# Block attention followed by a Fourier mixing layer: q and k of the last head pairs loaded in 32x32 blocks and turned on VectorE

## The chip, the cores and the metric

The kernel runs on one core of a Trainium2 chip. The metric is the device time of one execution in microseconds (us). The kernel before took 298.1 us, the median of three runs (297.7 to 298.16).

## What is computed

The reference has two halves, and the second works on the output of the first.

```python
# 1. block-sparse causal attention: B=4, H=8, S=768, D=64, blocks of 64 keys, top 3 blocks
k_rep = k.reshape(B, H, 12, 64, D).mean(axis=3)
gate  = einsum('bhsd,bhnd->bhsn', q, k_rep)          # which key blocks a query may see
mask  = (top-3 blocks of gate  |  own block) & causal
attn  = softmax(where(mask, q @ k.T / sqrt(D), -1e9))
x     = (attn @ v), heads side by side               # [4, 768, 512]
# 2. Fourier mixing and a two-layer net
mixed = real(fft(fft(x, axis=1), axis=2))
u     = x + mixed
un    = (u - mean(u)) / sqrt(var(u) + 1e-6)
out   = u + relu(un @ w_ch1) @ w_ch2                 # w_ch1 [512, 2048], w_ch2 [2048, 512]
```

## The kernel before

**Pairs and batches.** Attention is worked off in 16 head pairs `P` (0 to 15, four to a batch `b`). A pair is two heads of 64 numbers side by side, so that its transposed q and k fill 128 partitions. When the four pairs of a batch are done, the batch goes through the Fourier half and the two matrix products, W1 (16 steps `w:b,it`) and W2 (12 steps `c:b,st,h`). The attention of later batches is laid between the products of earlier ones.

**One order, written out by hand.** The string `ORDER` lists some thousand steps, each a short name with its arguments. The loop at the end calls them in that order, and the schedule is manual for all five queues (SyncE, called SP; TensorE, PE; VectorE, DVE; ScalarE, ACT; GpSimd, POOL). Each engine therefore works off its own instructions in the order in which the string names them and stops at the first one whose inputs are not there. Nothing reorders at run time. Between engines only semaphores hold.

**The steps of a pair.** `Lk`, `Lq` and `Lv` load k, q and v of a pair (function `load`, issued on SP: two DMAs each for k and q, line 275, one for v, line 270). The tile `nat0` (q) and `nat1` (k) hold tokens on the partitions and come in three buffers each. `tk` and `tq` (`a_tp`, line 292) turn them on PE: six transposes of 128x128 each against the identity, from fp32 SBUF into one PSUM tile `tp`. `ks` (line 297, DVE) sums k over each block of 64 tokens out of that PSUM tile; `kh` spreads the sums; `kc` (lines 308 and 311, ACT) writes k in fp16 into `qk`. `qc` (line 316, DVE) copies q from PSUM to the fp32 tile `q32`; `qs` (POOL) writes it in fp16 into `qk`. Then come the gate `g` (PE, from `q32` and the sums), the choice of blocks `gt`, `gx`, `gl`, `gm` (DVE), `K` (POOL, the mask rows of `qk`), the scores `s` (PE, lines 409 and 414), `e` (ACT, line 431, the exponential), `d` (POOL, line 437, the causal corner), `vc` (POOL, v to fp16), `v` (PE, line 449, attention times values) and `x` (DVE, the division).

**The steps of a batch.** `fs`, `fd`, `f` (DVE) fold `x`; `y` and `m` (PE) are the two Fourier products; `ty` (ACT) and `tr` (DVE, line 538) move the first product's result out of PSUM; `u` (DVE, line 566) adds; `xu` (ACT, line 578) centres the rows in fp16. `un` turns them into `unT`, for batch 0 by PE and DVE, for the other batches by two DMA transposes per step on the SP queue (line 593). `bn`, `nv`, `nr` are the statistics. `w` (PE, lines 629 and 631) is W1, `r` its ReLU (ACT, line 641; every fourth one DVE, line 639), `c` (PE, line 656, for the last piece line 648) is W2, `o` (DVE, line 668) adds, and `od` (SP, line 673) writes 128 rows of the output.

**Buffers that tie the queues together.** All PSUM tiles come from one pool of four. `u` has five buffers for three tiles a batch, so that later batches wait for earlier `od`. A DMA on SP takes one of eight completion lanes and waits until the DMA eight places before it has landed.

The part of the order that the change leaves as it is ends behind the first normalised rows of batch 0 (step `bn:0,3`); W1 of batch 0 begins there, some 59 us into the execution.

Of the kernel before, what the change touches and what calls it, by code (L numbers as in the profile page):

```python
# [116 lines left out]
qs:3 ks:3 s:1,4 e:1,0 tq:4 d:0,1 gx:2 vc:0 e:1,4 s:1,3 qc:4 s:1,1 Lv:2 e:1,3 s:1,2 gl:2,0 kh:3  # L117
tk:4 gl:2,1 e:1,2 d:1,3 gm:2 g:3 d:1,4 ks:4 d:1,0 v:0 d:1,5 gt:3 vc:1 kc:4 gx:3 e:1,1 s:2,5 Lv:3
Lq:6 LF:0 Lq:7 Lk:6 Lk:7 LT:0 s:2,3 kh:4 gl:3,0 e:2,5 gl:3,1 s:2,4 e:2,3 d:1,1 x:0 tq:5 qs:4 e:2,4
g:4 d:2,3 gm:3 qc:5 s:2,0 d:2,4 s:2,2 d:1,2 e:2,0 gt:4 d:2,5 tk:5 vc:2 gx:4 e:2,2 s:2,1 ks:5 d:2,0  # L120
Lv:4 Lq:8 Lk:8 s:3,1 e:2,1 v:1 gl:4,0 kh:5 gl:4,1 kc:5 d:2,1 gm:4 d:2,2 s:3,2 x:1 e:3,1 vc:3 g:5
e:3,2 Lv:5 Lc:0 d:3,1 s:3,5 gt:5 s:3,0 fs:0,1 e:3,5 s:3,3 d:3,2 gx:5 e:3,0 s:3,4 fs:1,1 tq:6
gl:5,0 e:3,3 fs:0,0 v:2 gl:5,1 fs:1,0 e:3,4 d:3,3 qc:6 d:3,0 s:4,5 x:2 d:3,4 s:4,4 e:4,5 d:3,5
s:4,0 qs:5 v:3 e:4,0 gm:5 fs:2,0 fs:2,1 e:4,4 s:5,5 x:3 s:4,1 e:5,5 s:5,1 e:4,1 fd:2,0 s:4,2 s:5,0
fs:3,1 e:5,1 fs:3,0 s:5,2 fd:2,1 e:5,0 fd:3,1 s:4,3 fd:3,0 e:5,2 tk:6 f:0,1 f:0,2 e:4,3 Lk:9 Lq:9
tk:7 f:0,3 e:4,2 f:0,0 y:0,1 ks:7 pg:0 W:0 kc:6 y:0,0 tr:0,1 d:4,0 kc:7 d:4,4 d:4,5 ks:6 d:5,5
d:4,1 ty:0,1 tr:0,0 s:5,3 d:5,2 s:5,4 d:4,3 kh:6 W:1 ty:0,0 m:0,2 qs:6 e:5,3 u:0,2 m:0,1 vc:4
e:5,4 m:0,0 u:0,1 xu:0,2 d:5,4 tk:8 d:5,1 d:4,2 u:0,0 xu:0,1 d:5,0 xt:0,2 W:2 g:6 un:0,2 xu:0,0
xt:0,1 gt:6 tq:8 un:0,1 kc:8 xt:0,0 qc:8 tq:7 un:0,0 qs:8 v:4 Lq:10 Lk:10 Lv:6 Lq:11 qc:7 bn:0,3
w:0,4 d:5,3 qs:7 bn:0,1 w:0,5 r:0,4 gx:6 ks:8 w:0,6 r:0,5 gl:6,0 kh:7 gl:6,1 x:4 w:0,7 r:0,6 gm:6  # L130
w:0,3 r:0,7 s:6,5 r:0,3 s:6,1 e:6,5 s:6,3 e:6,1 kh:8 s:6,2 fs:4,0 bn:0,4 w:0,2 e:6,2 d:6,1 X:0
e:6,3 g:7 w:0,0 d:6,5 gt:7 r:0,2 d:6,3 vc:6 gx:7 s:6,4 r:0,0 vc:5 s:6,0 e:6,4 tk:9 Li:0 gl:7,0
Lv:7 tq:9 gl:7,1 e:6,0 gm:7 w:0,11 Lq:12 Lv:8 K:7 qc:9 kc:9 g:8 r:0,11 v:5 gt:8 d:6,0 ks:9 w:0,8
qs:9 gx:8 w:0,10 x:5 r:0,8 d:6,4 d:6,2 gl:8,0 s:7,5 s:7,2 r:0,10 kh:9 fs:4,1 w:0,1 bn:0,5 e:7,5
vc:7 e:7,2 tq:10 gl:8,1 Lv:9 r:0,1 X:1 gm:8 s:7,4 qc:10 w:0,15 d:7,2 e:7,4 K:8 bn:0,0 g:9 r:0,15
s:7,0 w:0,9 gt:9 e:7,0 gx:9 vc:8 tq:11 r:0,9 d:7,0 Lv:10 s:7,1 qc:11 d:7,5 tk:10 d:7,4 e:7,1
gl:9,0 s:7,3 ks:10 v:6 e:7,3 kh:10 gl:9,1 kc:10 gm:9 d:7,3 s:8,4 bn:0,2 d:7,1 w:0,12 vc:9 x:6
e:8,4 K:9 Lv:11 Lk:11 Lq:13 Lq:14 Lk:12 Lk:13 v:7 r:0,12 g:10 x:7 s:8,3 w:0,13 e:8,3 gt:10 nv:0
s:9,4 r:0,13 fs:5,1 s:9,1 fs:7,0 vc:11 w:0,14 e:9,4 fs:6,1 e:9,1 fs:7,1 s:8,1 fs:6,0 fs:5,0
c:0,2,0 r:0,14 fd:7,1 fd:6,1 e:8,1 gx:10 s:9,0 fd:7,0 s:9,2 e:9,0 fd:6,0 s:8,2 gl:10,0 c:0,3,0  # L140
f:1,3 e:9,2 f:1,2 e:8,2 gl:10,1 f:1,0 s:8,0 gm:10 s:9,3 d:8,2 e:8,0 y:1,1 d:8,1 d:9,0 e:9,3 nr:0
c:0,0,0 tr:1,1 ty:1,1 s:9,5 c:0,2,1 e:9,5 d:8,0 d:9,3 tk:11 K:10 s:8,5 c:0,1,0 Lk:14 ks:11 kc:11
c:0,3,1 f:1,1 d:9,5 e:8,5 d:9,1 qs:10 tq:12 o:0,2 y:1,0 od:0,2 kh:11 d:8,4 o:0,3 pg:1 vc:10 qc:12
c:0,1,1 od:0,3 ty:1,0 d:9,4 Lv:12 Lv:13 qs:11 tr:1,0 g:11 c:0,0,1 gt:11 d:8,3 d:8,5 gx:11 qs:12
m:1,0 o:0,0 m:1,1 od:0,0 o:0,1 d:9,2 od:0,1 v:8 u:1,1 m:1,2 u:1,0 xu:1,1 c:0,4,0 gl:11,0 xu:1,0
un:1,1 x:8 s:10,3 gl:11,1 un:1,0 c:0,4,1 u:1,2 e:10,3 d:10,3 fs:8,0 s:10,5 s:10,2 bn:1,3 e:10,5
tk:12 e:10,2 fs:8,1 v:9 gm:11 Lk:15 Lq:15 ks:12 xu:1,2 K:11 bn:1,0 tq:13 kc:12 un:1,2 c:0,5,0
qc:13 vc:13 bn:1,4 s:11,2 d:10,5 x:9 s:11,4 vc:12 e:11,2 c:0,5,1 bn:1,1 Lv:14 Lv:15 e:11,4 s:11,0
o:0,5 s:11,5 w:1,11 e:11,5 od:0,5 o:0,4 e:11,0 kh:12 bn:1,5 od:0,4 s:11,3 w:1,7 e:11,3 r:1,11
s:10,1 d:11,3 r:1,7 d:11,0 s:10,0 e:10,1 d:11,4 g:12 d:10,2 tk:13 d:11,5 e:10,0 gt:12 d:11,2  # L150
s:11,1 ks:13 d:10,1 w:1,0 e:11,1 d:10,0 kh:13 fs:9,0 fs:9,1 s:10,4 r:1,0 d:11,1 gx:12 w:1,14
e:10,4 gl:12,0 gl:12,1 g:13 gm:12 r:1,14 d:10,4 w:1,12 K:12 gt:13 kc:13 gx:13 w:1,6 bn:1,2 r:1,12
tq:14 gl:13,0 r:1,6 qs:13 v:10 qc:14 gl:13,1 s:12,3 gm:13 s:12,5 v:11 x:10 e:12,3 K:13 e:12,5
s:12,0 x:11 w:1,8 e:12,0 fs:10,0 vc:15 s:12,1 r:1,8 s:12,2 fs:10,1 s:13,4 e:12,1 d:12,3 w:1,5
fs:11,1 d:12,5 e:13,4 fs:11,0 d:12,1 fd:10,0 w:1,10 r:1,5 fd:11,0 fd:10,1 s:13,0 fd:11,1 r:1,10
w:1,4 f:2,0 e:13,0 f:2,2 s:13,1 f:2,1 e:12,2 w:1,2 e:13,1 tk:14 r:1,4 w:1,3 ks:14 r:1,2 f:2,3
kc:14 s:12,4 kh:14 r:1,3 pg:2 y:2,0 d:13,4 vc:14 nv:1 e:12,4 qs:14 w:1,9 tr:2,0 w:1,13 ty:2,0
d:12,0 r:1,9 g:14 r:1,13 y:2,1 gt:14 gx:14 s:13,2 w:1,1 e:13,2 gl:14,0 gl:14,1 gm:14 s:13,5 w:1,15
tr:2,1 e:13,5 r:1,1 d:13,5 d:13,0 tk:15 ty:2,1 r:1,15 d:12,4 d:12,2 c:1,0,0 kc:15 nr:1 m:2,0 m:2,1
u:2,0 c:1,1,0 d:13,1 K:14 u:2,1 tq:15 ks:15 xu:2,1 s:13,3 bn:2,3 c:1,0,1 xu:2,0 un:2,1 qc:15  # L160
e:13,3 c:1,1,1 un:2,0 d:13,3 d:13,2 s:14,5 v:12 o:1,0 kh:15 od:1,0 o:1,1 v:13 e:14,5 bn:2,1 od:1,1
d:14,5 x:12 qs:15 s:14,3 m:2,2 e:14,3 bn:2,0 c:1,4,0 x:13 fs:13,0 g:15 fs:13,1 c:1,5,0 u:2,2
fs:12,0 xu:2,2 gt:15 c:1,2,0 bn:2,4 un:2,2 gx:15 c:1,5,1 gl:15,0 fs:12,1 gl:15,1 gm:15 bn:2,5
c:1,4,1 K:15 c:1,2,1 o:1,4 od:1,4 o:1,5 s:14,1 od:1,5 s:15,4 e:14,1 s:15,0 c:1,3,0 e:15,4 d:14,1
d:14,3 e:15,0 d:15,4 s:14,4 s:14,2 d:15,0 e:14,4 s:15,2 c:1,3,1 e:15,2 e:14,2 s:15,3 o:1,3 w:2,1
od:1,3 o:1,2 bn:2,2 w:2,2 od:1,2 r:2,1 s:15,5 w:2,4 e:15,5 w:2,15 r:2,4 r:2,2 w:2,3 r:2,15 e:15,3
s:15,1 r:2,3 d:15,3 w:2,9 d:14,4 e:15,1 d:14,2 d:15,2 d:15,5 s:14,0 r:2,9 d:15,1 w:2,14 e:14,0
v:15 d:14,0 w:2,5 x:15 w:2,7 r:2,5 fs:15,1 fs:15,0 r:2,14 fd:15,1 v:14 fd:15,0 r:2,7 w:2,6 x:14
w:2,11 fs:14,0 fs:14,1 fd:14,1 w:2,13 fd:14,0 f:3,2 f:3,0 w:2,10 r:2,13 r:2,11 w:2,8 f:3,3 r:2,10
f:3,1 nv:2 w:2,0 r:2,8 nr:2 r:2,6 y:3,1 r:2,0 y:3,0 ty:3,1 c:2,0,0 pg:3 tr:3,0 tr:3,1 w:2,12  # L170
c:2,1,0 r:2,12 ty:3,0 c:2,0,1 c:2,1,1 m:3,0 o:2,0 c:2,2,0 od:2,0 u:3,0 o:2,1 xu:3,0 m:3,1 od:2,1
c:2,4,0 u:3,1 un:3,0 xu:3,1 bn:3,2 m:3,2 c:2,3,0 u:3,2 un:3,1 bn:3,3 xu:3,2 c:2,5,0 bn:3,0 un:3,2
bn:3,5 c:2,3,1 bn:3,1 c:2,4,1 c:2,2,1 w:3,3 c:2,5,1 r:3,3 o:2,3 w:3,7 od:2,3 o:2,4 o:2,2 od:2,4
w:3,11 r:3,7 od:2,2 o:2,5 w:3,4 r:3,11 od:2,5 w:3,2 bn:3,4 nv:3 w:3,0 r:3,2 nr:3 w:3,8 r:3,0 w:3,1
r:3,8 w:3,13 r:3,1 r:3,4 w:3,6 w:3,10 w:3,9 r:3,10 r:3,13 w:3,5 r:3,6 w:3,14 r:3,5 w:3,12 c:3,2,0
r:3,12 r:3,9 r:3,14 c:3,0,0 w:3,15 c:3,4,0 r:3,15 c:3,1,0 c:3,0,1 c:3,1,1 c:3,5,0 o:3,0 od:3,0
o:3,1 c:3,3,0 od:3,1 o:3,5 od:3,5 c:3,4,1 c:3,2,1 o:3,4 od:3,4 c:3,3,1 c:3,5,1 o:3,3 od:3,3 o:3,2
od:3,2 o:3,6 od:3,6
# [5 lines left out]
def kernel(  # L184
# [9 lines left out]
    nc = tc.nc  # L194
    B, H, _, D = q.shape
# [5 lines left out]
    NPAIR = B * NP  # L201
    NSLOT = 3
    NVS = 4
    NX = 7

# [55 lines left out]
    pairs = [{} for _ in range(NPAIR)]  # L261
    x_t, u_t, un_t, h_t, st_t = {}, {}, {}, {}, {}

    def load(P, who):
        eng = nc.sync
        b, hp = divmod(P, NP)
        src = (q, k, v)[who]
        if who == 2:
            t = apool.tile([128, 2 * NST, 64], FP, tag="nat2", name=f"nat2_{P}", bufs=2)
            eng.dma_start(t, src[b, 2 * hp:2 * hp + 2].rearrange("e (st p) d -> p (e st) d", p=128))  # L270
            nat[P, 2] = t
            return
        t = apool.tile([128, NST, 2, 64], FP, tag=f"nat{who}", name=f"nat{who}_{P}", bufs=3)
        for e in range(2):
            eng.dma_start(t[:, :, e, :],
                          src[b, 2 * hp + e].rearrange("(st p) d -> p st d", p=128))
        nat[P, who] = t
# [8 lines left out]
    def a_tp(P, who):  # L286
        d = pairs[P]
        d["slot"] = P % NSLOT
        d["tp", who] = ps = pst([128, S], f"tp{who}_{P}")
        src = nat[P, who].rearrange("p st e d -> p st (e d)")  # L290
        for st in range(NST):
            nc.tensor.transpose(ps[:, 128 * st:128 * st + 128], src[:, st, :], id32)  # L292

# [19 lines left out]
    def a_q32(P):  # L313
        q32 = apool.tile([128, S], FP, tag="q32", name=f"q32_{P}")
        pairs[P]["q32"] = q32
        nc.vector.tensor_copy(out=q32, in_=pairs[P]["tp", 0])  # L316
# [471 lines left out]
```

## Time and profile before

| what | value |
|---|---|
| median of three runs | 298.1 us (297.7 to 298.16) |
| span of the profiled execution | 295.6 us; the median lies 2.5 us above it |
| PE busy | 286.5 us, 97% |
| DVE, ACT, POOL busy | 192.5 (65%), 164.2 (56%), 111.1 (38%) us |
| granted PE clock | 1.00 throughout |
| DMA | 33.53 MB in 93200 packets, of which 85936 under 512 B |

The profiled execution's own device time is not listed apart from the three runs; the 2.5 us are what lies around the span, by the median. "Busy" of PE counts modelled ends of pipelined matmuls, so a busy PE is read together with the chain of waits. A chain is followed back from the last instruction: at each step to what released it, or to the instruction before it on its engine.

### The profile page before, as it was taken

How to read it: one execution, taken by the hardware profiler on the slowest of the kernel's cores; microseconds unless marked ns; L12 is line 12 of the kernel's file. 1: busy time of each engine (PE TensorE's matmuls, PEld its weight loads, DVE VectorE, ACT ScalarE, POOL GpSimd, SP SyncE). 2: the span in 40 equal slices, each digit the busy share in tenths (PEclk: the TensorE clock that was granted, in tenths of full speed). 3: DMA queues.
4: the chain of work that ended last, by engine and by line, in shares of the span. 5: the costliest groups of instructions: out<-in, count | busy, mean ns of one | idle time of the engine just before them, and what ended most of it. 6: DMA issues, size and time to landing. Idle time of an engine off the chain costs nothing.

```text
span 295.6 us, 6738 instructions
## 1 busy us (share of the span) xinstructions
PE 286.5 (97%) x2633; PEld 180.2 (61%) x2633; DVE 192.5 (65%) x597; ACT 164.2 (56%) x205; POOL 111.1 (38%) x286
## 2 busy tenths in 40 slices
PE   8899999999999999999999999999999999999995
PEld 4566767765676556656757667446666554555453
DVE  2999999986988638987796577714493282700132
ACT  3698989749578841677788843165524250155000
POOL 2267528528776289064753363220303000110000
PEclk9999999999999999999999999999999999999999
DMA  8999999997999727477000005311000052300023
GB/s 197 268 228 230 262 245 199 195 230 118 226 185 211 168 55 186 118 164 176 3 0 2 0 9 136 38 72 71 2 1 2 32 103 44 142 0 2 0 91 125
DMA packets 93200, 33.53 MB, mean 113 GB/s; under 512 B 85936, under 2 KB 89968, under 8 KB 93168
## 3 DMA queue, kind: packets, MB, share of 16 engines
q1 hardware_dynamic: 87504, 28.47, 40.6%
q0 software_dynamic: 3664, 4.19, 9.1%
q10 hardware_dynamic: 2000, 0.44, 0.7%
q8 instruction: 21, 0.34, 0.5%
q14 instruction: 11, 0.09, 0.1%
HBM read 28.63 MB, written 6.29 MB: 118 GB/s over the span
## 4 chain that ended last, share of the span: by engine, by line
PE 84%; DVE 7%; ACT 6%; DMA 1%; issue 1%; DVEq 0%; ACTq 0%
PE c L656 26%; PE h L629 19%; PE h L631 10%; PE sc L414 7%; PE av L449 6%; ACT pt L431 5%; PE tp L292 5%; PE yp L519 2%; PE mx L552 2%; DVE q L316 2%; PE mx L553 1%; PE warmps L693 1%; DVE u L566 1%; PE g L342 1%; PE c L648 1%; PE sc L409 1%
## 5 line engine op out<-in xcount | busy, mean ns | idle before, releaser
L431 ACT ACTIVATE pt<-sc 128x1024 f16<-128x1024 f32 (+1 forms) x96 | 83.3, 923 | 26.6 <-PE sc L414 19.7
L629 PE MATMUL h<-unT,w 128*128 128x512 f16 x256 | 85.1, 379 | 0.0
L656 PE MATMUL c<-w_sb,hT 128*128 128x512 f16 x368 | 83.8, 379 | 0.0
L631 PE MATMUL h<-unT,w 128*128 128x256 f16 x256 | 69.7, 272 | 0.4 <-DMA unT<-x 0.4
L641 ACT ACTIVATE hT<-h 128x768 f16<-128x768 f32 x48 | 37.8, 813 | 43.7 <-PE h L631 43.7
L656 PEld LDWEIGHTS <-hT 128*128 128x128 f16 x368 | 35.6, 98 | 39.3 <-issue 0.5
L437 POOL TENSOR_SCALAR_AFFINE_SELECT pt<-pt 128x256 f16<-128x256 f16 x96 | 37.5, 414 | 58.5 <-ACT pt L431 57.6
L629 PEld LDWEIGHTS <-w 128*128 128x128 f16 x256 | 25.0, 97 | 29.2 <-issue 1.3
L668 DVE SCALAR_TENSOR_TENSOR u<-c,rs,u 128x512 f32<-128x512 f32 (+1 forms) x25 | 17.5, 725 | 31.2 <-PE c L656 30.4
L639 DVE TENSOR_SCALAR hT<-h 128x768 f16<-128x768 f32 x16 | 15.3, 955 | 29.7 <-PE h L631 29.6
L578 ACT ACTIVATE x<-u,nm 128x512 f16<-128x512 f32 x24 | 15.9, 715 | 22.5 <-DVE nm L572 22.3
L292 PE MATMUL tp<-id,nat 128*128 128x128 f32 x192 | 27.5, 284 | 0.6 <-ACT pt L431 0.3
L631 PEld LDWEIGHTS <-w 128*128 128x128 f16 x256 | 25.0, 98 | 4.3
L225 POOL TENSOR_SCALAR_AFFINE_SELECT qk<-mt 32x160 f16<-32x160 f16 x72 | 23.1, 341 | 10.8 <-DVE mt L386 9.1
L414 PE MATMUL sc<-qk 96*128 96x512 f16 (+3 forms) x144 | 26.8, 305 | 0.0
L225 POOL TENSOR_SCALAR_AFFINE_SELECT qk<-q 64x768 f16<-64x768 f32 (+1 forms) x25 | 20.6, 825 | 14.8 <-DVE q L316 14.1
L292 PEld LDWEIGHTS tp<-id,nat 128*128 128x128 f32 x192 | 22.2, 146 | 5.7 <-issue 1.6
L449 PE MATMUL av<-v,pt 128*128 128x65 f16 x672 | 23.0, 193 | 0.1
L449 PEld LDWEIGHTS <-pt 128*128 128x128 f16 x672 | 22.0, 97 | 1.7 <-POOL pt L437 0.5
L297 DVE TENSOR_REDUCE kr<-tp 128x12 f32<-128x768 f32 x16 | 15.1, 945 | 5.9 <-PE tp L292 5.9
L222 POOL TENSOR_TENSOR t<-vr,rs 128x6 f32<-128x6 f32 x12 | 2.4, 199 | 43.5 <-DVE rs L609 42.9
L414 PEld LDWEIGHTS <-qk 96*128 96x128 f16 x144 | 13.3, 97 | 8.9 <-issue 0.5
(95 smaller groups left out, 351.2 us busy)
## 6 DMA issues: line engine op xcount, KB each, us to landing
nat<-in_v_dram SPq DMA_DIRECT2D x16, 384.0 KB, 4.7
nat<-in_k_dram SPq DMA_DIRECT2D x31, 192.0 KB, 3.5
nat<-in_q_dram SPq DMA_DIRECT2D x31, 192.0 KB, 3.9
out_dram<-u SPq DMA_DIRECT2D x23, 256.0 KB, 2.1
w_sb<-in_moe_w_ch_dram POOLq DMA_DIRECT2D x2, 1024.0 KB, 10.2
w<-in_moe_w_ch_dram POOLq DMA_DIRECT2D x2, 768.0 KB, 8.4
fs_sb<-c_FS SPq DMA_DIRECT2D x1, 582.0 KB, 5.1
w<-in_moe_w_ch_dram POOLq DMA_DIRECT2D x1, 512.0 KB, 7.3
```

The costliest lines, as they stand in the source:

```text
L225: nc.gpsimd.affine_select(out=out, in_=in_, pattern=[[0, i] for i in n], base=0, channel_multiplier=0, compare_op=ALU.is_ge, fill=0.0)
L292: nc.tensor.transpose(ps[:, 128 * st:128 * st + 128], src[:, st, :], id32)
L414: nc.tensor.matmul(ps[:, e, co:co + q1 - q0], qk[0:96, e, 1, 128 * jt:128 * jt + 128], qk[0:96, e, 0, q0:q1], start=True, stop=True)
L431: nc.scalar.activation(out=d["pt"][:, o:o + 2 * n].rearrange("p (e c) -> p e c", e=2), in_=d["sc", i][:, :, 0:n], func=AF.Exp, scale=0.125)
L437: nc.gpsimd.affine_select(out=dg, in_=dg, pattern=[[0, 2], [1, 128]], base=0, channel_multiplier=-1, compare_op=ALU.is_ge, fill=0.0)
L449: nc.tensor.matmul(av[:, e, 66 * st:66 * st + 65], pt[:, co:co + 128], vv[:, e, jt, 0:65], start=(cnt == 0), stop=(cnt == 20))
L578: nc.scalar.activation(out=x_b[:, 2 * kp + k2, :], in_=u_b[:, k2, :], func=AF.Identity, scale=0.0625, bias=nm[:, k2:k2 + 1])
L629: nc.tensor.matmul(hp[:, 0:512], w1s, unT[:, dt, 0:512], start=(dt == 0), stop=(dt == NDT - 1))
L631: nc.tensor.matmul(hp[:, 512:768], w1s, unT[:, dt, 512:768], start=(dt == 0), stop=(dt == NDT - 1))
L641: nc.scalar.activation(out=hT, in_=hp, func=AF.Relu)
L656: nc.tensor.matmul(c_ps[b, g[0]][:, st - g[0], :], h_t[b, it][:, 128 * st:128 * (st + 1)], w2_sb[:, it, :], start=(it == 0), stop=(it == N ...
L668: nc.vector.scalar_tensor_tensor(out=o, in0=ps, scalar=st_t[b][1][:, st:st + 1], in1=o, op0=ALU.mult, op1=ALU.add)
```

## The change

From pair 9 on for q (seven pairs) and from pair 11 on for k (five pairs) the load has another form. Each of four DMAs brings the tokens of one half of one head (32 of the 64 numbers) to 32 partitions: token `32 n + r` goes to partition `32 g + r`, columns `32 n` to `32 n + 31`, in runs of 32 fp32 numbers, 128 B (before: two DMAs with runs of 64 numbers, 256 B). One DVE transpose in 32x32 blocks of the 128x768 tile then gives what the six PE transposes gave. For q it takes the place of the copy out of PSUM in `qc`; for k a new step `kb` does it in place in `nat1`, and `ks` and `kc` read that SBUF tile instead of PSUM. The steps `tq:9` to `tq:15` and `tk:11` to `tk:15` are gone.

```diff
+    BLK = (range(9, NPAIR), range(11, NPAIR))
...
     def load(P, who):
...
         t = apool.tile([128, NST, 2, 64], FP, tag=f"nat{who}", name=f"nat{who}_{P}", bufs=3)
+        nat[P, who] = t
+        if P in BLK[who]:
+            nat[P, who] = t = t.rearrange("p st e d -> p (st e d)")
+            for g in range(4):
+                eng.dma_start(t[32 * g:32 * g + 32].rearrange("p (n c) -> p n c", c=32),
+                              src[b, 2 * hp + g // 2, :, 32 * (g % 2):32 * (g % 2) + 32]
+                              .rearrange("(n r) c -> r n c", r=32))
+            return
         for e in range(2):
             eng.dma_start(t[:, :, e, :],
                           src[b, 2 * hp + e].rearrange("(st p) d -> p st d", p=128))
-        nat[P, who] = t
...
+    def k_turn(P):
+        pairs[P]["tp", 1] = t = nat[P, 1]
+        nc.vector.transpose(out=t, in_=t)
...
     def a_q32(P):
...
-        nc.vector.tensor_copy(out=q32, in_=pairs[P]["tp", 0])
+        if P in BLK[0]:
+            nc.vector.transpose(out=q32, in_=nat[P, 0])
+        else:
+            nc.vector.tensor_copy(out=q32, in_=pairs[P]["tp", 0])
...
-        "tk": lambda P: a_tp(P, 1), "tq": lambda P: a_tp(P, 0), "ks": a_sums, "kh": a_half,
+        "tk": lambda P: a_tp(P, 1), "tq": lambda P: a_tp(P, 0), "kb": k_turn, "ks": a_sums, "kh": a_half,
```

Behind `bn:0,3` the string `ORDER` is new. Except for the twelve steps taken out and the five put in, it names the same steps in another order, on every queue. These are two stretches of it, picked out by queue. PE, from the first W1 product of batch 0 to the first of batch 1:

```
before: w:0,4 w:0,5 w:0,6 w:0,7 w:0,3 s:6,5 s:6,1 s:6,3 s:6,2 w:0,2 g:7 w:0,0 s:6,4 s:6,0 tk:9 tq:9
 w:0,11 g:8 v:5 w:0,8 w:0,10 s:7,5 s:7,2 w:0,1 tq:10 s:7,4 w:0,15 g:9 s:7,0 w:0,9 tq:11 s:7,1 tk:10
 s:7,3 v:6 s:8,4 w:0,12 v:7 g:10 s:8,3 w:0,13 s:9,4 s:9,1 w:0,14 s:8,1 c:0,2,0 s:9,0 s:9,2 s:8,2
 c:0,3,0 s:8,0 s:9,3 y:1,1 c:0,0,0 s:9,5 c:0,2,1 tk:11 s:8,5 c:0,1,0 c:0,3,1 tq:12 y:1,0 c:0,1,1 g:11
 c:0,0,1 m:1,0 m:1,1 v:8 m:1,2 c:0,4,0 s:10,3 c:0,4,1 s:10,5 s:10,2 tk:12 v:9 tq:13 c:0,5,0 s:11,2
 s:11,4 c:0,5,1 s:11,0 s:11,5 w:1,11
after:  w:0,0 w:0,7 w:0,2 w:0,4 w:0,6 g:7 s:6,1 s:6,5 s:6,2 s:6,0 w:0,8 w:0,11 g:8 s:6,3 s:6,4 v:5 tk:9
 s:7,1 w:0,14 s:7,0 w:0,13 w:0,3 s:7,2 g:9 s:7,3 s:7,4 w:0,5 tk:10 w:0,15 s:7,5 w:0,1 w:0,10 w:0,12
 v:6 w:0,9 v:7 s:9,3 s:8,3 c:0,2,0 s:9,5 s:8,1 g:10 c:0,2,1 c:0,3,0 s:8,2 s:8,0 s:9,4 c:0,3,1 s:9,1
 y:1,0 y:1,1 c:0,0,0 s:8,4 c:0,0,1 s:8,5 m:1,1 c:0,1,0 m:1,0 s:9,0 s:9,2 c:0,1,1 m:1,2 c:0,4,0 g:11
 s:10,0 v:8 s:10,3 c:0,5,0 s:10,4 c:0,4,1 s:10,2 s:10,5 v:9 s:10,1 c:0,5,1 s:11,4 w:1,14
```

SP, from `Lk:11` to its end:

```
before: Lk:11 Lq:13 Lq:14 Lk:12 Lk:13 Lk:14 od:0,2 od:0,3 Lv:12 Lv:13 od:0,0 od:0,1 un:1,1 un:1,0
 Lk:15 Lq:15 un:1,2 Lv:14 Lv:15 od:0,5 od:0,4 un:2,1 un:2,0 od:1,0 od:1,1 un:2,2 od:1,4 od:1,5 od:1,3
 od:1,2 od:2,0 od:2,1 un:3,0 un:3,1 un:3,2 od:2,3 od:2,4 od:2,2 od:2,5 od:3,0 od:3,1 od:3,5 od:3,4
 od:3,3 od:3,2 od:3,6
after:  Lk:11 od:0,3 od:0,2 Lq:13 Lq:14 Lk:12 Lk:13 un:1,1 un:1,0 Lk:14 un:1,2 Lv:12 od:0,5 od:0,1
 od:0,0 Lv:13 Lk:15 Lq:15 Lv:14 od:1,1 od:1,0 od:0,4 od:1,5 un:2,1 Lv:15 un:2,0 un:2,2 od:1,2 od:1,4
 od:2,0 od:2,1 od:1,3 un:3,0 un:3,1 un:3,2 od:3,0 od:2,3 od:2,2 od:3,5 od:3,4 od:2,4 od:3,3 od:3,2
 od:2,5 od:3,1 od:3,6
```

And the steps between which the prediction counts elsewhere, in the order after. DVE: `x:7 qc:10 fs:6,1 fd:6,1 gt:10 fs:7,1 fd:6,0 fs:7,0 fd:7,1 fd:7,0 f:1,2 gx:10 f:1,3 gl:10,0 f:1,0 f:1,1 o:0,3 o:0,2`, and later `u:1,1 u:1,0 bn:1,3 u:1,2`, with all five `kb` between `gm:10` and `ks:15`. ACT: `xu:1,1 e:9,0 e:9,2 xu:1,2 xu:1,0`. PE in batch 2: `c:1,0,0 s:13,3 c:1,1,0 s:12,2 s:13,4 s:12,1 c:1,0,1 y:2,0`, and `m:3,2 c:2,2,1 c:2,3,0 c:2,3,1 c:2,4,1 w:3,1`.

## The prediction

> **What bounds the kernel now.** I read the page first: busy time by engine and the forty slices.
>
> ```profile
> PE 286.5 (97%) x2633; PEld 180.2 (61%) x2633; DVE 192.5 (65%) x597; ACT 164.2 (56%) x205; POOL 111.1 (38%) x286
> ...
> PE   8899999999999999999999999999999999999995
> ...
> DVE  2999999986988638987796577714493282700132
> ```
>
> PE is full from the third slice on and the others are not. As ends of matmuls are modelled, that alone proves little, so the chain of waits comes second: its shares, then its pieces in order of time.
>
> ```profile
> PE 84%; DVE 7%; ACT 6%; DMA 1%; issue 1%; DVEq 0%; ACTq 0%
> ```
>
> From 58.7 us (the end of `v:4`, where the new order begins) to 292.2 us every piece of the chain is PE work, one after the other without a gap, but for one place, just ahead of the first W1 product of batch 1:
>
> ```profile
> 127.36 1.73 PE c L656 x8
> 129.09 0.45 PE sc L414 x2
> ...
> 129.62 0.71 ACT pt L431
> 130.32 2.45 DMA unT<-x
> 132.78 0.04 issue
> 132.82 0.27 PE h L631
> ```
>
> PE has nothing to do from 129.54 to 132.82 us, 3.3 us, until the last DMA transpose of batch 1 lands. So behind 58.7 us the time is PE's work plus 3.3 us. The busy times by stretch say who could take PE's place (PE, PEld, DVE, ACT, POOL, clock, DMA share, GB/s):
>
> ```profile
> 58.70:95.80 37.10, 37.10 (x400) 24.36 (x397) 30.82 (x114) 25.65 (x32) 24.04 (x53) 1.00 1.00 193
> 95.80:132.80 37.00, 36.64 (x300) 22.28 (x298) 27.19 (x85) 21.04 (x29) 20.58 (x52) 1.00 0.61 139
> 132.80:169.00 36.20, 36.18 (x333) 24.28 (x333) 27.12 (x94) 28.81 (x35) 17.77 (x42) 1.00 0.16 38
> 169.00:200.00 31.00, 31.00 (x247) 17.39 (x245) 18.61 (x59) 13.69 (x18) 12.38 (x39) 1.00 0.28 61
> ```
>
> DVE is next, at 83, 73, 75 and 60%; DMA is full only up to some 100 us.
>
> **PE work taken out.** The instructions of `tp` behind 58.7 us are 84 matmuls, 14 turns of six; `tk:9` and `tk:10` stay. The chain has them all: ten of 0.66 us, two together 1.46, one 0.69, one 0.81.
>
> ```profile
> 70.80 1.46 PE tp L292 x12
> ...
> 157.37 0.66 PE tp L292 x6
> ```
>
> Together 9.56 us; less the two that stay (0.73 + 0.66) that is 8.1 us, all on the path. The instructions' own mean of 273 ns overlaps and would give 20 us for 72; the chain's 110 ns count.
>
> **DVE work put in.** The trace has block transposes of 160 and 288 columns, and the copy that `qc` drops:
>
> ```profile
> L349 DVE STREAM_TRANSPOSE gt<-g 128x288 f32<-128x288 f32 x7 | 3.3, 473 | 0.0
> ...
> L354 DVE STREAM_TRANSPOSE gt<-g 128x160 f32<-128x160 f32 x9 | 3.1, 346 | 3.5 <-PE g L342 3.4
> ...
> L316 DVE COPY q<-tp 128x768 f32<-128x768 f32 x16 | 15.1, 945 | 3.6 <-PE tp L292 3.5
> ```
>
> 128 columns more cost 127 ns, so 768 columns cost 473 + 480 x 0.99 = 0.95 us. For q that replaces 0.945 us: nothing. For k, five times 0.95 = 4.75 us are new. They lie between about 104 and 155 us, where DVE has some 19 us idle in 73, and I take their cost on the path as nothing; cover gone, 4.75 us. Each `kb` also waits for its load, with the next pairs' sums, `u:1,1` and `o:0,0` queued behind it on DVE: by the count further down, k of 11 is issued at about 96 us and wanted at 105, k of 12 issued at 110 and wanted at 119, against a landing of some 4 us (the median of q and k loads is 3.5 and 3.9), so those waits are nothing. The lower bound is below nothing: `kb` and `qc` need a load that is long there, no longer a PE turn (DVE waited 5.9 and 3.5 us for those). The Trainium skill ("VectorE: DVE Perf Modes", the three transpose paths) gives 311 ns for 128x128 in bf16 on VectorE and 390 on TensorE; the rows here have 110 ns of PE's time for such a turn and 0.16 us of DVE's for 128 columns. By the page's figure a 768-column turn would be 6 x 0.311 = 1.87 us and DVE would gain 15.8 us in place of 4.75; the rows decide.
>
> `ks` reads SBUF instead of PSUM at an unknown difference; the nearest rows are ACT's: 715 ns for 512 columns out of SBUF (line 578), against 595 interpolated downwards from 813 for 768 and 1030 for 1024 out of PSUM. So some 0.12 us for each of ten `kc` and five `ks`, 1.8 us on engines at 56 and 65%; between nothing and that, I take nothing on the path.
>
> **Loads.** Each new load has 4 issues instead of 2 and 3072 packets instead of 1536. SP takes a median of 0.63 to 0.65 us an issue; its unpressed pairs took 1.13, so 0.6. That is 1.2 us more per load on SP. No row has 128 B packets: the hardware queue's 87504 packets in 40.6% of 16 engines' span make 21.9 ns each. If bytes set the time, a load costs what it did; if packets do, 1536 x 21.9 / 16 = 2.1 us of all engines more. Four loads (q of 9 to 12) fall into the stretch with DMA share 1.00: 0 to 8.4 us. Their cover: q of 12 is issued at about 73 us and turned past 104; the W2 halves go out at about 73 and 79, need 10.2 us and are read at 91 and 94. So 6 us and more, and I take nothing. The Trainium skill ("DMA: Bandwidth & Descriptors", how a descriptor splits into AXI transactions; why small descriptors are slow) speaks against the change: a read starts at a 256 B boundary, so the upper 128 B of a row cost as many beats as the whole row, with 3 cycles on each packet: 7 and 11 cycles where a 256 B packet has 11. That would make a load 18/11 of what it was, an estimate, between my two bounds.
>
> **The new order, at its tightest place.** I count PE from 58.7 us by the chain's pieces (`w` 1.30, `c` 1.73, `v` 1.28, `g` 0.41, a wide score tile 0.43, narrow 0.11, `y` 1.1, `m` 0.88). Up to `v:7`: 16 `w` 20.8, three `g` 1.2, scores of pairs 6 and 7 2.3 + 2.3, three `v` 3.8, `tk:9` and `tk:10` 1.3: 90.5 us. Up to `m:1,2`: eight `c` 13.8, `g:10`, scores 4.1, two `y`, three `m`: 114.1 us. Up to `w:1,14`: four `c` 6.9, `g:11`, two `v` 2.6, scores 2.7: 126.7 us.
>
> Against that SP. `x:7` ends at 91.7; `gt:10` waits for `g:10` at 94.0; three folds (0.39 + 0.39 and differences of 0.6 three times, to 97.0), four `f` and the maxima (4.1) lead to 101.1, where PE wants `y:1,0` at 100.9: 0.2 us lost. `o:0,3` and `o:0,2` at 0.75 give 102.6, their `od` 103.3. Now four loads, 16 issues at 0.6: 112.9. `un:1,1` (2.44) to 115.3. `un:1,0` waits for ACT: `m:1,2` 114.1, `u` 1.6, `xu:1,2` and `xu:1,0` 1.43 each, 118.6; it ends at 121.0. Load of k 14: 123.4. The second transpose of `un:1,2` goes out at 124.6 and lands 2.5 us later, 127.1; with the slowest landing of such a transpose, 4.1, at 128.7. PE is there at 126.7: 0.4 to 2.0 us, I take 1.0. So the 3.3 us of before mostly go, and the same wait is next late.
>
> In batch 3, `m:3,2` to `w:3,1` has four `c`, 6.9 us; before, the last transpose (issued 244.9, landing 2.5) came 7.2 us behind `m:3,2` at 240.2: 0.3 us. `K:9` for `s:9,3` and the last `d` of pair 10 for `v:10` come within 1 us of PE by the same count, and DVE is dense around `f:2`: 1.5 us in all as an estimate, bounds 0 and 5. The end is as before: the last `od` waits for the last `c`, the others are out by then.
>
> **Sum**, against the profiled span: 295.6 - 8.1 - 3.3 + 0.2 + 1.0 + 0.3 + 1.5 = 287.2 us. With the 2.5 us around it, 289.7 us.
>
> **Rivals.**
> - DVE becomes the bound. For it: 83% in one stretch and dense work ahead of `y:2,0`. Against: no DVE wait of 1 us stands in PE's chain behind 58.7. If all 4.75 us come on the path, 294.4; up to 297.4 with the 1.5 at its bound of 5 as well, rounded down.
> - Slower: SP and the block loads hold up `un:1,2`. It stands behind 20 block DMAs. With d us for each, the landing is 103.3 + 16 d + 4.9 + 4 d + 3.7 = 111.9 + 20 d; the whole gain of 11.4 us is gone at 138.1, d = 1.3, 27 ns for each of 48 packets per engine. At 21.9 ns d is 1.05: landing 132.9, 6.2 us of wait, 284.2 + 6.2 + 2.0 + 2.5 = 294.9, still faster. At d = 1.5 it is 15.2 us of wait and 303.9. For it: short packets into 32 partitions are new here. Against: their bytes are half.
> - The gain isn't PE's: PE would refill the time with waits up to the old 298.1. Only several of the above together do that.
> - No waits at all: 295.6 - 11.4 + 2.5 = 286.7.
>
> **Numbers.** The forecast, waits of 0 to 5 us in all, 286.7 to 292: 0.63. DVE or packets late but still faster, up to 297.4: 0.18. Within 0.2% (0.6 us, about what a measurement of this kernel can tell from no change): 0.03. Slower through the loads: 0.16. The range 286.5 to 296.5 leaves out the slower case and the end of the second.
>
> **What would show it.** `tp` with 120 matmuls in all; twelve block transposes of 768 columns at 0.95 us; the chain all PE behind 58.7 us; a wait of about 1 us for `unT` ahead of the first W1 product of batch 1, at about 127 us; block DMAs 0.6 us apart on SP. Wrong if that wait passes 5 us, if transposes take near 2 us, or if the chain shows DVE or POOL pieces between 95 and 200 us.

## The result, and the profile after

The changed kernel takes 304.4 us (median of four, 304.0 to 305.5) against 297.9 for the kernel before beside it. The ratio is 1.0236, 95% interval 1.0206 to 1.0265 (the two medians alone give 1.022): slower, where I had forecast 289.7 us. The profiled execution spans 303.3 us. It is the slowest of the four (305.5 us); the three others span 301.9, 301.9 and 302.7.

The page of the kernel after: busy times, PE's and DVE's slices, then the chain's shares.

```profile
PE 280.8 (93%) x2561; PEld 172.7 (57%) x2561; DVE 199.5 (66%) x602; ACT 164.8 (54%) x205; POOL 111.4 (37%) x286
...
PE   7799999999979999999999997999999999999980
...
DVE  2999899996868987887998348840491636421040
...
PE 67%; DVE 17%; ACT 9%; issue 3%; SPq 1%; DMA 1%; DVEq 0%; ACTq 0%
```

PE has 72 instructions less, but holes that it did not have (the 7 in slices 12 and 25), and it is done a whole slice before the span ends (the 0). DVE has gained 7 us and is far from full.

To place the holes I matched PE's matmuls, which are in the order of the string, to their steps, and took from the time between two steps' starts the time that a step of its kind usually takes before. From 58.6 us on PE loses 1.9 us that way before and 11.9 after. From PE's last matmul to the end of the span it is 3.7 us before and 9.3 after. So 295.6 - 7.9 (72 matmuls of 110 ns) + 10.0 + 5.6 = 303.3 us. Some 1.4 of the 10.0 are no wait but a slower clock behind one (last section).

The two largest of PE's waits in the timeline of after (start, duration, instruction, in brackets the idle time ahead of it and its releaser):

```profile
89.04 0.38 PE L641 MATMUL h<-unT,w 128*128 128x512 f16 x1 [2.20 <-ACT qk L320]
...
188.31 1.12 PE L461 MATMUL av<-v,pt 128*128 128x65 f16 x31 [1.89 <-POOL pt L449]
```

The first is `w:0,12`. It waits for a PSUM tile until the one of `tk:10` is read out. The chain of waits of after shows by whom:

```profile
84.53 0.85 DVE sd L221
85.38 0.77 DVE ltb L221
...
86.17 0.34 DVE mt L398
86.52 0.85 DVE kr L306
...
87.39 0.79 ACT qk L320
...
88.20 0.80 ACT qk L320
...
89.04 0.38 PE h L641
```

`ks:10` (kr) stands behind a fold, `gl:9,1` and `gm:9` on DVE, and `kc:10` (qk) starts only when `ks:10`, the other reader of that tile, has ended. The second wait is `v:12`. It needs the causal corners `d` of pair 12, and POOL's timeline says why these are late:

```profile
179.62 2.68 POOL L224 TENSOR_SCALAR_AFFINE_SELECT qk<-mt 32x160 f16<-32x160 f16 x8 [11.06 <-DVE mt L398]
182.36 1.84 POOL L449 TENSOR_SCALAR_AFFINE_SELECT pt<-pt 128x256 f16<-128x256 f16 x5
```

POOL stands 11 us at `K:14`, which waits for `gm:14`, and eleven `d` are queued behind it. The end, first in DVE's timeline of after:

```profile
292.52 3.78 DVE L680 SCALAR_TENSOR_TENSOR u<-c,rs,u 128x512 f32<-128x512 f32 x6 [11.51 <-PE c L668]
```

then in SP's:

```profile
293.30 6.21 SPq L685 DMA_DIRECT2D out_dram<-u  x11
```

and in SP's before:

```profile
251.83 41.19 SPq L673 DMA_DIRECT2D out_dram<-u  x11
```

Before, the last eleven outputs leave over 41 us. After, all eleven leave in the last 6: `o:3,0` is first of six on DVE and waits for `c:3,1,1`, as rows 0 and 1 share a PSUM tile; `od:3,0` waits for it on SP, and the outputs of batch 2, ready since some 258 us, stand behind `od:3,0`.

### The profile page after: what moved, and what is told of

It is laid out like the page before. It is cut to its first block, busy times and chain, and to the rows that moved or that the text cites. A ratio compares the mean times of both kernels' runs of the same rounds, so it can differ in the third digit from the quotient of the medians.

```text
span 303.3 us, 6618 instructions
## 1 busy us (share of the span) xinstructions
PE 280.8 (93%) x2561; PEld 172.7 (57%) x2561; DVE 199.5 (66%) x602; ACT 164.8 (54%) x205; POOL 111.4 (37%) x286
## 4 chain that ended last, share of the span: by engine, by line
PE 67%; DVE 17%; ACT 9%; issue 3%; SPq 1%; DMA 1%; DVEq 0%; ACTq 0%
PE c L668 21%; PE h L641 16%; PE h L643 8%; PE sc L426 5%; PE av L461 5%; ACT pt L443 4%; DVE u L578 3%; DVE u L680 2%; ACT qk L320 2%; PE tp L297 2%; DVE kr L306 2%; PE yp L531 2%; DVE q L328 1%; PE warmps L705 1%; DVE tr L550 1%
## 5 line engine op out<-in xcount | busy, mean ns | idle before, releaser
L461 PE MATMUL av<-v,pt 128*128 128x65 f16 x672 | 24.2, 196 | 2.3 <-POOL pt L449 1.9
L461 PEld LDWEIGHTS <-pt 128*128 128x128 f16 x672 | 23.1, 99 | 5.2 <-POOL pt L449 2.5
L578 DVE SCALAR_TENSOR_TENSOR u<-mx,x 128x512 f32<-128x512 f32 x24 | 15.6, 687 | 5.5 <-PE mx L565 5.3
L426 PEld LDWEIGHTS <-qk 96*128 96x128 f16 x144 | 13.2, 98 | 10.3 <-issue 2.2
L297 PE MATMUL tp<-id,nat 128*128 128x128 f32 x120 | 17.1, 281 | 1.1 <-DMA nat<-in_k_dram 0.4
L610 DVE BATCH_NORM_STATS2 bst<-u 128x6 f32<-128x512 f32 x24 | 16.2, 675 | 0.0
```

The costliest lines, as they stand in the source:

```text
L426: nc.tensor.matmul(ps[:, e, co:co + q1 - q0], qk[0:96, e, 1, 128 * jt:128 * jt + 128], qk[0:96, e, 0, q0:q1], start=True, stop=True)
L461: nc.tensor.matmul(av[:, e, 66 * st:66 * st + 65], pt[:, co:co + 128], vv[:, e, jt, 0:65], start=(cnt == 0), stop=(cnt == 20))
L578: nc.vector.scalar_tensor_tensor(out=u_b[:, k2, :].rearrange("p (m two) -> p two m", two=2), in0=mps[:, k2, :].rearrange("p (two m) -> p t ...
```

## The experiments

Theory: the loss is made by the new order, in these places; loads and turns are cheap. Rival: the block loads, or the turns on VectorE, cost what was lost. Times are medians; each ratio, with its 95% interval, is to the kernel before, run beside it (it differs by up to 0.2% from the quotient of the medians).

**The turns and loads in the old order (e1).**

```diff
 ORDER as before, but
-tq:9 ... tq:15   tk:11 ... tk:15
+kb:11 ... kb:15   (each where its tk stood)
```

> The block loads and VectorE's turns in the order of before (tq of pairs 9 to 15 left out, kb where tk of pairs 11 to 15 stood). My theory: the loss sits in the new order, so here the 72 turn matmuls go for 72 x 0.11 = 7.9 us and PE's 1.9 us of lost time stay about what they were: 298 - 7.9 = 290 us, 288.5 to 293. Rival, the blocks themselves (short packets, SP's issues, 4.75 us more on VectorE) cost what after lost: no gain, 298 to 306 us.

306.3 us, 1.0312 (1.0265 to 1.036). The theory fell as I had put it: without the new order the change is slower still. PE loses 18 us, most of it in two places of its timeline:

```profile
97.68 2.11 PE L426 MATMUL sc<-qk 96*128 96x512 f16 x6 [6.30 <-POOL qk L224]
...
142.41 0.27 PE L643 MATMUL h<-unT,w 128*128 128x256 f16 x1 [4.06 <-DMA unT<-x]
```

POOL's timeline of the same run leads to a load:

```profile
92.87 0.90 POOL L224 TENSOR_SCALAR_AFFINE_SELECT v<-nat 128x768 f16<-128x768 f32 x1 [4.71 <-DMA nat<-in_v_dram]
93.83 0.30 POOL L404 MEMSET qk<- 32x256 f16 x1
94.09 4.21 POOL L224 TENSOR_SCALAR_AFFINE_SELECT qk<-mt 32x160 f16<-32x160 f16 x8
```

POOL's timeline of before has the same cast and the same copies:

```profile
88.48 0.90 POOL L225 TENSOR_SCALAR_AFFINE_SELECT v<-nat 128x768 f16<-128x768 f32 x1
...
89.71 2.67 POOL L225 TENSOR_SCALAR_AFFINE_SELECT qk<-mt 32x160 f16<-32x160 f16 x8
```

SP's timeline of e1 leads to other loads:

```profile
134.18 2.06 SPq L277 DMA_DIRECT2D nat<-in_k_dram  x4
...
138.64 2.52 SPq L605 DMA_TRANSPOSE unT<-x  x2
```

In the stretch where the DMA engines are full (share 0.99 from 80 to 100 us, with 172 GB/s against 207 before) the v load of pair 9 lands at 92.9 us, and `K:9` stands behind its cast `vc:9`, which starts 4.4 us later than before. `K:9` itself is slower too: its eight copies take 4.2 us where before they took 2.7; why was not separated. Later the k load of pair 15 waits for a k buffer until 134.2, since `kc:12` now reads that buffer itself, and the two transposes of `un:1,2` stand behind its and q's eight issues.

**The same order with plain loads (e7), and the new order with plain loads (e8).**

```diff
-        if P in BLK[who]:
-            (four block DMAs)
         for e in range(2):
             eng.dma_start(t[:, :, e, :], ...)
+        if P in BLK[who]:
+            nat[P, who] = t.rearrange("p st e d -> p (st e d)")
```

> The old order with VectorE's turns (as in the first run of a set, 306.2 us), but these twelve loads taken as before: two issues, 256-byte packets, so the tiles' content is arranged wrongly and the products are of other numbers; turns and order the same. Theory: PE's 6.5 us ahead of s:9,4 (v loads landing late in the stretch of full DMA, the cast of pair 11 ahead of K:9 on POOL) and 4.7 us ahead of s:11,3 (un:1,2 behind the loads of pair 15) come from the block loads' packets and issues: 291 to 297 us. Rival, VectorE's turns and their places make it slow: 303 to 307 us.

294.4 us, 0.9886 (0.985 to 0.9922). The twelve turns are on VectorE as in e1, and the kernel is 1.1% faster than before. So in the old order the turns are worth it, and the block loads cost 306.3 - 294.4 = 11.9 us.

> After with the same plain loads (content arranged wrongly, turns and order the same). If the new order covers the block loads, as I hold, nothing changes: 303.5 to 305 us. If their packets and issues cost in the new order too: 299 to 302 us.

304.6 us, 1.0201 (1.0164 to 1.0239). In the new order the block loads cost nothing that can be measured (304.4 us with them): it covers them, and pays elsewhere.

**Repairs of the new order, one at a time.** The end (e3), and the part of it on SP alone (e12):

```diff
 ORDER of after, e3
-... c:3,5,0 c:3,0,1 c:3,4,0 c:3,4,1 c:3,3,1 o:3,5 c:3,2,1 c:3,1,0 c:3,1,1 o:3,0 o:3,4 o:3,3 o:3,2 o:3,1
- c:3,5,1 o:3,6 od:3,0 od:2,3 od:2,2 od:3,5 od:3,4 od:2,4 od:3,3 od:3,2 od:2,5 od:3,1 od:3,6
+... c:3,1,0 c:3,0,1 c:3,1,1 c:3,5,0 o:3,0 od:3,0 o:3,1 od:3,1 c:3,4,0 c:3,4,1 o:3,5 od:3,5
+ c:3,3,1 c:3,2,1 o:3,4 od:3,4 c:3,5,1 o:3,3 od:3,3 o:3,2 od:3,2 o:3,6 od:3,6
+ (and od:2,2 to od:2,5 ahead of w:3,9; this line alone is e12)
```

> After with only its end put in another order: c:3,1,0 and c:3,1,1 around c:3,0,1, then o:3,0 and o:3,1 and the rest as their products come; od:2,2 to od:2,5 behind o:2,3. My theory: from PE's last matmul to the span's end after has 9.34 us, before 3.74; that wait is o:3,0's (one PSUM tile shared with c:3,1,1) and od:2's behind od:3,0 on SP; it goes, 304.4 - 5.6 = 298.8 us, 298 to 300. Rival, the 11 late outputs are late because the block loads or the queue are slow: no change, 303.5 to 304.5.

299.6 us, 1.0073 (1.0052 to 1.0094). PE's last matmul to the end is 3.7 us again, and the DVE timeline has the outputs spread:

```profile
287.68 0.75 DVE L680 SCALAR_TENSOR_TENSOR u<-c,rs,u 128x512 f32<-128x512 f32 x1 [2.90 <-PE c L668]
291.14 1.41 DVE L680 SCALAR_TENSOR_TENSOR u<-c,rs,u 128x512 f32<-128x512 f32 x2 [2.70 <-PE c L668]
```

> After with od:2,2 to od:2,5 alone moved on SP, from behind od:3,0 to ahead of w:3,9 (about 255 us); o:3,0 and the six others still wait on VectorE for c:3,1,1. It splits the 4.8 us that the other order of the end brought. If the queue on SP is most of it: six outputs of VectorE are through at 296.3 us, the last seven od issued by then and landed 2.4 us later, so some 4 us go: 300 to 301 us. If VectorE's wait is most of it: at most 1.5 us go, 303 us or more.

301.9 us, 1.0121 (1.0051 to 1.019), between the two expectations. In its profile 6.5 us remain behind PE's last matmul, against 9.3 and 3.7: half of the end's loss is the queue on SP, half the wait on VectorE.

```diff
 ORDER of after, e4
-d:12,2 K:14 d:12,0 ... d:12,4 vc:13 qs:15 K:15
+d:12,2 d:12,0 ... d:12,4 vc:13 K:14 qs:15 K:15
```

> After with K:14 alone moved on POOL's queue, from behind d:12,2 to behind d:12,4 and vc:13. My theory: POOL's 11 us of waiting for gm:14 at K:14 hold up the selections of pairs 12 and 13, and v:12 with them; without it some 2 of the 4 us that PE loses between 185 and 193 us go, up to all 4 if the dip of the granted clock goes with them: 300.4 to 302.5 us. Rival, VectorE's four k turns ahead of that place are late and PE waits there anyway: no change, 303.8 to 304.6.

303.0 us, 1.0212 (1.0186 to 1.0237): a gain of 1.4, less than expected. Its interval overlaps that of after (1.0206 to 1.0265), so the gain rests on the trace. There the wait ahead of the rest of `v:12` is gone, and 0.7 us ahead of `s:14,2` come in its place, for the same `K:14`, plus 0.7 ahead of `s:15,1`.

```diff
 ORDER of after, e5
-tk:9 x:5 kc:9 ... ks:9 ... gl:9,0 qc:11 ... s:7,5 e:7,5 ... ks:10 ... kc:10
+tk:9 ks:9 x:5 kc:9 ... gl:9,0 ks:10 qc:11 ... s:7,5 e:7,5 kc:10 ...
```

> After with ks:9 straight behind tk:9, ks:10 ahead of qc:11 and kc:10 behind e:7,5, nothing else moved. My theory: the PSUM tiles of tk:9 and tk:10 are held until sums and copy have read them, from 74 to 89 us, and PE lacks a tile for w:0,13 and w:0,12: 0.7 + 2.4 us and some of the 0.9 behind them go, 300.5 to 302 us. Rival, the loads of 128-byte packets make these pairs late: no change, 303.8 to 304.6.

301.8 us, 1.0159 (1.0144 to 1.0174), as expected. On the queues only the two sums have moved, both on VectorE; `kc:10` follows `e:7,5` on ACT in after too. Of the two tiles, that of `tk:10` made the gain: PE's loss ahead of `w:0,13` only moved to `s:7,0`, which now waits for `x:5`.

**The three together (e6).**

> After with the three repairs together (end, K:14, sums and copies of pairs 9 and 10). My theory: three separate waits, so the gains add: 304.4 - 4.8 - 1.4 - 2.6 = 295.6 us, 294.5 to 297, just under the 297.3 of before. Rival: what is cured in one place is waited for in the next, so 298 us or more.

295.6 us, 0.9916 (0.9891 to 0.9941): the gains add, and the new order is now 0.8% faster than before. PE still loses 7.7 us, most of it in thirteen places of 0.2 to 0.8.

**More moves, for most of these places (e9).**

```diff
 ORDER of e6
+ tk:9 ks:9 ahead of v:5; bn:0,4 bn:0,0 behind gt:9; y:1,1 ty:1,1 tr:1,1 ahead of y:1,0; c:1,2,1 ahead of s:15,1
+ v:13 ahead of s:14,2; c:2,2,1 ahead of o:2,0; o:0,4 behind c:0,5,1; o:0,0 behind c:0,1,1; o:1,1 ahead of f:2,2
+ Lk:14 behind un:1,2
```

> The three repairs of after (295.6 us) and eleven more moves, each for a wait of PE of 0.2 to 0.8 us in that run's trace: tk:9 ahead of v:5, bn:0,4 and bn:0,0 behind gt:9, y:1,1 ahead of y:1,0 with its copies, c:1,2,1 ahead of s:15,1, v:13 ahead of s:14,2, c:2,2,1 ahead of o:2,0, o:0,4 and o:0,0 behind the second halves of their tiles, o:1,1 ahead of f:2,2, the k load of pair 14 behind un:1,2. If the waits are separate, some 6.1 us of PE's 7.7 us of lost time go: 289.5 us, 289 to 291.5. If each only moves on to the next meeting: 294 us or more.

300.3 us, 1.0088 (1.007 to 1.0107): a miss, 4.7 us worse than e6. PE loses 12.4 us, at other steps. One of them in its timeline:

```profile
133.75 0.48 PE L354 MATMUL g<-q,krb 128*32 128x160 f32 x8 [1.07 <-DVE u L680]
```

`g:12` waits for an output `o` on VectorE that I had not counted, and so does `y:1,0` (1.5 us). Which move did which harm I did not separate.

**The 3.3 us of my sum (e0).** In the kernel before:

```diff
 ORDER of before
-un:1,1 x:8 ... un:1,0 ... Lk:15 Lq:15 ... un:1,2
+un:1,1 x:8 ... un:1,0 un:1,2 ... Lk:15 Lq:15 ...
-   (... , x_t[b][:, kt, :])
+   (... , x_t[b][:, kt - 2 * ((b, kp) == (1, 2)), :])
```

> Before with the two DMA transposes of un:1,2 straight behind un:1,0 on SP; they turn rows 256 to 511 of x in place of rows 512 to 767 (so part of the result is another), which are ready earlier. It prices the 3.3 us of my sum. By the chain as I read it in the prediction, PE is idle from 129.54 to 132.82 us: 297.3 - 3.3 = 294.0 us. By a count of PE's own steps, that loses only 0.5 us ahead of w:1,11: 296.5 to 297.2 us.

297.4 us, 0.9982 (0.9967 to 0.9997): 0.5 us, not 3.3.

**The old order, repaired (e10, e11).** e1's two waits have one step each in front of them. e10 is one move, e11 adds two:

```diff
 ORDER of e1
-vc:9 x:6 e:8,4 K:9          (e10)
+K:9 vc:9 x:6 e:8,4
-Lk:15 Lq:15 ks:12 xu:1,2 K:11 bn:1,0 kc:12 un:1,2      (e11, with e10)
+ks:12 xu:1,2 K:11 bn:1,0 kc:12 un:1,2 Lk:15 Lq:15
-gl:11,1 un:1,0 ... v:9 gm:11
+gl:11,1 gm:11 un:1,0 ... v:9
```

> The old order with block loads (306.2 us) with K:9 ahead of vc:9 on POOL, nothing else. There PE lost 6.5 us ahead of s:9,4: K:9 stood behind vc:9, which waited for its v load until 92.9 us. Theory: the load is late, not K:9's own data; with K:9 in front the 6.5 us go, and some 1 to 2 us behind them where the granted clock was 0.7: 298 to 300 us. Rival, gm:9 is late as well or s:9,4 waits for another thing next: 303 to 306 us.

298.1 us, 0.9992 (0.9967 to 1.0017): some 8 us for one step moved on POOL.

> The same with two moves more: the q and k loads of pair 15 behind un:1,2 on SP (they stood ahead of it, waiting for kc:12 to free a k buffer, and issue 8 block DMAs at 0.53 us), and gm:11 straight behind gl:11,1 on VectorE (K:11 waits for it, s:11,2 for K:11). Theory: of the 4.7 + 0.7 us at the first W1 products of batch 1 and the 1.4 us ahead of s:11,2 most goes: 6 us under the run with K:9 alone, 291.5 to 294.5 us, so under before's 297.5. Rival, un:1,2 is late by ScalarE's copies and not by the loads: less than 3 us under it.

290.5 us, 0.9769 (0.9739 to 0.98), 7.6 us under e10, 1 us better than the best that I expected, and faster than both kernels. What each of the two added moves brought was not separated. Its page:

```profile
PE   8799999999999999999999999999999999999995
...
PE 75%; DVE 16%; ACT 6%; issue 1%; DVEq 0%; ACTq 0%
```

PE loses 2.9 us there, 1.0 more than before, and the span is 288.7 = 295.6 - 7.9 + 1.0. In SP's timeline the transposes of `un:1,2` now follow `un:1,0` at once:

```profile
117.35 8.62 SPq L605 DMA_TRANSPOSE unT<-x  x6
```

## Why the prediction was wrong, step by step

The sum gave a span of 287.2 us, the profile 303.3: 16.1 us apart. They are -7.9 for -8.1 (0.2), nothing for -3.3 (3.3), 10.0 us of new losses of PE for my 3.0 (7.0) and 5.6 us at an end that I had as unchanged (5.6).

- **PE work taken out, -8.1: right.** `tp` has 120 matmuls, and the span of e11, 6.9 us under before with 1.0 us more lost, fits the chain's 110 ns.
- **"PE has nothing to do from 129.54 to 132.82 us": wrong.** The chain left PE there for ACT and a DMA, and I took that for an idle PE. The timeline of before shows PE at work on a product and two score tiles all that while:

```profile
129.79 1.89 PE L656 MATMUL c<-w_sb,hT 128*128 128x512 f16 x8
131.52 0.71 PE L414 MATMUL sc<-qk 96*128 96x512 f16 x4
...
132.82 0.27 PE L631 MATMUL h<-unT,w 128*128 128x256 f16 x1 [0.38 <-DMA unT<-x]
```

  The wait was the 0.38 in the bracket; e0 prices it at 0.5 us.
- **DVE work put in: right in size, and hidden.** Groups of after by shape:

```profile
L326 DVE STREAM_TRANSPOSE q<-nat 128x768 f32<-128x768 f32 x7 | 6.8, 965 | 0.9 <-POOL qk L224 0.9
...
L301 DVE STREAM_TRANSPOSE nat<-nat 128x768 f32<-128x768 f32 x5 | 4.8, 957 | 0.0
...
L320 ACT CAST qk<-nat 64x768 f16<-64x768 f32 x10 | 8.3, 827 | 0.2
```

  0.96 us for the forecast 0.95; e7 and e11 carry all twelve and are faster than before. Reading k from SBUF cost 9 ns for `ks` (947 against 938) and 33 for `kc` (827 against 794), not 120.
- **Loads taken at nothing: right for this order, and only for it.** The issues took 0.5 to 0.6 us. A 128 B packet took 13.2 ns in the mean of the trace's records and a 256 B packet 18.7, so a block load costs 1.41 times as much, 0.7 us of all engines more. The Trainium skill ("DMA: Bandwidth & Descriptors", how a descriptor splits into AXI transactions), from which I had estimated 18/11 = 1.64, has the direction right and overstates the size here. It would make the upper half of a row dearer than the lower (11 cycles and 7); of the 128 B packets in the trace 81% took 13 ns and 13% took 11, and no half of them is longer than the other. The cover of 6 us and more was no reason to take nothing, though: e1 and e7 show 11.9 us of cost in the old order, not through the late q tile that I had looked at, but through v loads and DMA transposes queued behind.
- **The tightest place, 1.0 us: the size right, the times not.** `w:1,14` lost 0.4 us for `unT`. The last transpose landed at 132.9 us, not 127.1 to 128.7, and PE came there at 132.3, not 126.7: both were late, for the most part by what had been lost ahead. The 0.2 us at `y:1,0` were 0.2.
- **"1.5 us in all as an estimate, bounds 0 and 5": the step that failed most.** The places I named (`K:9`, `v:10`) cost nothing measurable; PE lost 10.0 us more than before, nearly all of it at places I had not walked through: PSUM tiles held by `ks` and `kc` (up to 3.9 us by `v:7`; e5 brought 2.6), `K:14` on POOL (4 us with the fall of the clock behind it; e4 brought 1.4), and a dozen of 0.2 to 0.8. I had followed PE and SP through the new order, but not DVE's and POOL's queues, where a step stands behind another whose input is late.
- **"The end is as before": wrong, 5.6 us.** I had checked that the last `od` waits for the last `c`, but not what stands behind the first. e3 gives back 4.8.
- **Rivals.** The slower case, block DMAs ahead of `un:1,2`, did not happen; nor did DVE become the bound. Nearest was the third, that PE refills the time with waits, but I had capped it at the old 298.1. The kernel was slower by a mechanism that I had not made a rival: the waits of the new order itself, which I had bounded at 5 us, and its end. In the old order the loads did bite ahead of `un:1,2`, by 4.1 us (e1), through a buffer that is held longer and not through 27 ns a packet (13.5 ns in e1).
- **Signs.** Of the three that I had named for being wrong, one came: the chain of after has DVE pieces between 95 and 200 us, from `tr` at 108.82 to `u` at 189.55. The wait for `unT` and the turns stayed far below their limits.
- **Two slips in the working, neither decisive.** The upper end of the DVE rival is 289.7 + 4.75 + 3.5 = 297.95, not 297.4. With `y` at the 1.1 of my list, PE is at `m:1,2` at 113.7 us; the 114.1 hold with the 1.0 and 1.5 us that the two `y` take in the trace of before.

That 290.5 us of e11 lie near my 289.7 is luck and no merit of the sum: the -3.3 that was not there, 3.0 us of waits where 1.0 came, and 1.8 us around the span in place of 2.5 nearly cancelled.

## What to carry to other kernels

A chain of waits tells one path; whether the bounding engine was idle is read from that engine's own timeline (e11's chain is 16% DVE, and PE misses 2.9 us). When a change comes with a new order, walk every in-order queue through it, look for each step that waits long and list what stands behind it, and count buffers, PSUM tiles too, by their last reader. A change that frees the bounding engine can be worth its full price in the old order once the two or three steps that it makes late are moved; here three moves (e11) did better than a wholly new order.

## What the hardware showed that I had not expected

**The granted clock after a short wait.** In after, `v:12` and `v:13` stood 1.9 and 0.4 us idle, and from 190 to 193 us the clock was 0.50 (window of after: PE, PEld, DVE, ACT, POOL busy, clock, DMA share, GB/s):

```profile
190.00:193.00 3.00, 2.76 (x44) 2.49 (x45) 2.90 (x8) 2.53 (x3) 2.77 (x8) 0.50 0.39 61
```

`v:13` took 2.49 us there and the score tile behind it 0.95. In e3, with the same two waits at the same time (1.90 and 0.38 us), the clock stayed at 1.00 and they took 1.46 and 0.60. So 1.4 us of after's loss came with the clock. It came and went between executions of the same kernel as well, it seems: the four of after have a mean clock of 0.987, 0.986, 0.992 and 0.991, and span 303.3, 302.7, 301.9 and 301.9 us (only the first has a trace). The Trainium skill ("TensorE: Matmul & The Clock Gate", Part 1) puts the fall behind an idle window of some 3.4 us; here about 2 us sufficed in one run and not in another.

**fp16 operations of DVE that end with POOL's.** Ahead of `ks:10` in after, a fold took 0.93 us where its mean is 0.39 us, and `gl:9,1` took 0.84 where six of the nine such steps take 0.20 to 0.22 (they are the first two pieces of the chain above), while POOL ran two copies, in its timeline:

```profile
84.34 1.72 POOL L224 TENSOR_SCALAR_AFFINE_SELECT qk<-q 64x768 f16<-64x768 f32 x2
```

In the trace the two copies end at 85.16 and 86.06 us, and DVE's two operations at 85.38 and 86.14, 0.22 and 0.08 us behind them. It isn't new with the change: in the traces of before and after five `gl:P,1` of eighteen took 0.79 to 0.93 us, and each of the five began while POOL ran such a copy, of q or v, and ended 65 to 77 ns behind it. The Trainium skill ("SBUF — State Buffer", who interferes with whom) describes a port pair of DVE and GpSimd that is an exclusive lock, and has a DVE instruction with two SBUF inputs contend with a GpSimd one that reads SBUF. That fits; no run here separated it. It is 1.2 us of the 2.2 that `w:0,12` waited.
